# Splitting the last expert's second product into two column halves with their own sums, and swapping two PSUM banks between turns

## The chip, the core and the metric

The kernel runs on one core of a Trainium2 chip. The core has a matrix engine (TensorE; PE in the rows, PEld for its weight loads), a vector engine (VectorE; DVE), a scalar engine (ScalarE; ACT), a general engine (GpSimd; POOL) and a synchronising engine that issues most transfers (SyncE; SP). The metric is device time in microseconds (us) of one execution; the profile's rows are times inside one profiled execution, counted from the start of its span. Matmul results land in PSUM, which has eight banks of 2 KB in each of 128 partitions; a bank holds 512 fp32 columns.

## The reference, cut to what matters

Three stages follow one another: attention over (2, 8, 768, 64) with sink tokens and a window of 128; a dense feed-forward layer of 512 to 2048 to 512 on the 1536 tokens; and a routed layer with eight experts, of which each token goes to one. Only the last stage is touched here:

```python
logits = x @ w_gate
expert_idx = np.argmax(logits, axis=1)
...
h = np.maximum(np.einsum('ecd,edf->ecf', disp, w1), 0.0)
y = np.einsum('ecf,efd->ecd', h, w2)
out[i] = gate_w[i] * y[expert_idx[i], pos[i]]
```

An expert has `w1` of 512 x 1024 and `w2` of 1024 x 512, and takes at most 384 tokens.

## The kernel before, in words

Every fp32 product is made of fp32r products: an operand is cut into a high part (`h`, a rounded copy made by ScalarE) and a low part (`l`, the difference, made by VectorE), and the products high times high, high times low and low times high are summed in PSUM. The weights of the experts come from memory in pieces of 128 x 512 (L1274), are cut (L1291 or L1289 the high part, L1293 the low part) and wait in buffers named `cw`.

The routed tokens of each expert lie in a queue in memory, in units of 128. The experts are worked on one after another, as eight groups, in an order set by the number of tokens. For the first four groups the program holds arms for one, two or three units, chosen by a branch on the number of tokens; the execution profiled takes arms with two or three units. An arm is `group` (L1598):

- each unit's tokens are turned by TensorE (four transposes, `turn`, L1410) into a bank, and cut from there by ScalarE and VectorE (`x_parts`, L1416 and L1417) into `xt`. Unit 0 of the next group is turned early, while the group before is at work, into the tile `px`. Unit 1 is turned at the start of its group into `ph3`, and unit 2 into `px`; in the first group, whose units 0 and 1 were done ahead, only unit 2 is turned, into `ph3`;
- the first product (`up`, L1429) into the four tiles `ph0` to `ph3`, with ReLU and cutting (`h_parts`, L1438 and L1439) into `ht`;
- the second product (`down`, L1478) into the tiles `py0`, `py1` and `py2`, one for each unit;
- the multiplication by the gate (`out`, L1486) into `ys`, and an indirect DMA from GpSimd's queue (L1487) to the tokens' rows of the output.

The last four groups have few tokens. One runs as `lone` (one unit), and three as `half` (L1573), with at most 64 tokens each. In a half group the 128 stationary columns of a matmul are 64 high parts and 64 low parts, so that two products (with the weights' high and low part) do the work of three; the result's rows 0 to 63 and 64 to 127 must be added at the end. The steps of `half` for group gi are: the first product (L1531), 16 matmuls of 512 columns into `ph0` and `ph1`; a copy (L1534) to `hs`; `half_turn` (L1541), which turns `hs` and adds its two halves; ReLU and cutting (L1544, L1545); the second product `half_down` (L1552), 16 matmuls of 512 columns in one accumulation into one bank, `py0` or `py1` by the parity of gi; and `half_out`, in which ScalarE multiplies rows 64 to 127 by the gate into `hs` (L1561), VectorE multiplies rows 0 to 63 by the gate and adds (L1562), and GpSimd issues the output's indirect DMA (L1564). `half_next` turns the next half group's tokens into `px`.

The order of the work on every engine in this part is the order in which the code is written. The eight banks are `ph0` to `ph3`, `py0` to `py2` and `px`. `ph3`, `py1`, `py2` and `px` are opened after the routing's own four banks are closed; `ph3` takes the bank in which the first group's unit 1 was turned, `px` the bank of an earlier routing step.

## Time and profile before

| what | value |
|---|---|
| median of 3 runs | 599.1 us (596.08, 599.1, 600.12) |
| the profiled execution | 597.57 us |
| span of its rows | 595.8 us |
| TensorE matmul busy | 567.0 us (95%) |
| VectorE busy | 340.1 us (57%) |
| ScalarE busy | 288.2 us (48%) |
| GpSimd busy | 189.0 us (32%) |
[...]

The span is what the engines' rows cover; the execution's own time is 1.77 us longer. Each busy share is an average over all stages. In the page's strip of 40 slices (14.9 us each) TensorE stands at 8 or 9 tenths in every slice but the last, where it stands at 4.

### The profile page before, as it was taken

How to read it: one execution, taken by the hardware profiler on the slowest of the kernel's cores; microseconds unless marked ns; L12 is line 12 of the kernel's file. 1: busy time of each engine (PE TensorE's matmuls, PEld its weight loads, DVE VectorE, ACT ScalarE, POOL GpSimd, SP SyncE). 2: the span in 40 equal slices, each digit the busy share in tenths (PEclk: the TensorE clock that was granted, in tenths of full speed). 3: DMA queues.
4: the chain of work that ended last, by engine and by line, in shares of the span. 5: the costliest groups of instructions: out<-in, count | busy, mean ns of one | idle time of the engine just before them, and what ended most of it. 6: DMA issues, size and time to landing. Idle time of an engine off the chain costs nothing. (4 is left out here: it accounts for less than half of the span.)

```text
span 595.8 us, 11536 instructions
## 1 busy us (share of the span) xinstructions
PE 567.0 (95%) x3925; PEld 492.5 (83%) x3925; DVE 340.1 (57%) x814; ACT 288.2 (48%) x836; POOL 189.0 (32%) x304
## 2 busy tenths in 40 slices
PE   8879899999999999999999999999899999999994
PEld 7656677889888888898889889987698988988783
DVE  4999996554444344434444522475467666646992
ACT  4737576744345444444454423453434444424771
POOL 5328799722422242224222332141202010001110
PEclk9969899999999999999999999999989999999998
DMA  8979996834174022220240037562375765444940
GB/s 228 251 223 297 315 275 193 254 109 143 65 219 124 19 68 73 92 55 14 68 129 14 5 111 269 179 214 70 109 238 181 240 222 172 156 153 131 324 157 10
DMA packets 83562, 91.87 MB, mean 154 GB/s; under 512 B 42963, under 2 KB 51155, under 8 KB 83472
## 3 DMA queue, kind: packets, MB, share of 16 engines
q1 hardware_dynamic: 81488, 85.68, 46.9%
q0 software_dynamic: 1984, 5.13, 2.4%
q8 instruction: 39, 0.64, 0.4%
q14 instruction: 51, 0.42, 0.3%
HBM read 72.01 MB, written 20.09 MB: 155 GB/s over the span
## 5 line engine op out<-in xcount | busy, mean ns | idle before, releaser
L1010 PE MATMUL y<-wh,gp 128*128 128x512 f32 x360 | 131.2, 405 | 0.7 <-ACT gp L990 0.7
L992 POOL TENSOR_TENSOR gp<-g,gp 128x256 fp32r<-128x256 f32 x81 | 60.7, 749 | 189.2 <-ACT gp L990 180.9
L981 DVE TENSOR_TENSOR g<-hps,g 128x256 f32<-128x256 f32 x84 | 35.4, 422 | 109.8 <-ACT g L980 106.2
L964 PE MATMUL hps<-xth,wh 128*128 128x256 f32 x320 | 91.7, 287 | 0.4 <-DVE g L981 0.4
L964 PE MATMUL hps<-xtl,wh 128*128 128x256 f32 x320 | 90.1, 282 | 0.0
L964 PE MATMUL hps<-xth,wl 128*128 128x256 f32 x320 | 90.0, 281 | 0.0
L1293 DVE TENSOR_TENSOR cw<-craw,cw 128x512 fp32r<-128x512 f32 x128 | 84.0, 699 | 9.2 <-ACT cw L1291 8.0
L1010 PEld LDWEIGHTS y<-wh,gp 128*128 128x128 f32 x360 | 67.6, 188 | 15.3 <-ACT gp L990 1.1
L1291 ACT CAST cw<-craw 128x512 fp32r<-128x512 f32 x112 | 63.4, 621 | 23.7 <-PE py L1478 23.1
L980 ACT ACTIVATE g<-hps 128x256 f32<-128x256 f32 x84 | 32.2, 383 | 79.5 <-PE hps L964 78.3
L1010 PE MATMUL y<-wl,gp 128*128 128x512 f32 x180 | 70.4, 391 | 0.0
L1478 PE MATMUL py<-cw,ht 128*128 128x512 f32 x264 | 64.0, 398 | 0.3 <-DVE ht L1466 0.3
L964 PEld LDWEIGHTS hps<-xth,wh 128*128 128x128 f32 x320 | 60.3, 188 | 3.4 <-DVE g L981 0.9
L964 PEld LDWEIGHTS hps<-xtl,wh 128*128 128x128 f32 x320 | 60.3, 188 | 2.4
L964 PEld LDWEIGHTS hps<-xth,wl 128*128 128x128 f32 x320 | 60.6, 189 | 0.0
L1429 PE MATMUL ph<-xt,cw 128*128 128x256 f32 (+2 forms) x444 | 59.2, 295 | 1.1 <-DVE xt L1417 1.1
L1429 PEld LDWEIGHTS ph<-xt,cw 128*128 128x128 f32 x444 | 58.0, 194 | 1.4 <-DVE xt L1417 1.3
L1478 PEld LDWEIGHTS py<-cw,ht 128*128 128x128 f32 x264 | 49.0, 189 | 11.7 <-DVE ht L1466 0.9
L990 ACT CAST gp<-g 128x256 fp32r<-128x256 f32 x84 | 34.5, 410 | 30.9 <-DVE g L981 29.7
L1487 POOL DMA_INDIRECT out<-ys,gt x11 | 11.4, 1034 | 115.2 <-DVE ys L1486 109.7
L562 ACT ACTIVATE pm<-pm,mx 128x132 f32<-128x132 f32 (+1 forms) x80 | 31.6, 400 | 13.6 <-DVE mx L553 13.6
L1010 PEld LDWEIGHTS y<-wl,gp 128*128 128x128 f32 x180 | 34.0, 189 | 3.9
(222 smaller groups left out, 1007.2 us busy)
## 6 DMA issues: line engine op xcount, KB each, us to landing
craw<-in_moe_w SPq DMA_DIRECT2D x128, 256.0 KB
rawi<-in_moe_w_in SPq DMA_DIRECT2D x16, 512.0 KB
rawo<-in_moe_w_out SPq DMA_DIRECT2D x16, 512.0 KB
places<-zero SPq DMA_DIRECT2D x24, 257.0 KB
wh<-wscr SPq DMA_DIRECT2D x16, 256.0 KB
wl<-wscr SPq DMA_DIRECT2D x16, 256.0 KB
xg<-places SPq DMA_DIRECT2D x12, 257.0 KB
natv<-in_v SPq DMA_DIRECT2D x12, 256.0 KB
```

Source lines behind the costliest of these rows:

```text
L562: self.nc.scalar.activation(a, a, AF.Exp, bias=mx[:, pr, e:e + 1], accum_out=su[:, pr, e:e + 1])
L964: nc.tensor.matmul(ps, lhsT=w, rhs=x, start=(n == 0), stop=(n == len(mm) - 1))
L980: nc.scalar.activation(g, ps, AF.Copy, scale=0.01)
L981: nc.vector.tensor_tensor(out=g, in0=ps, in1=g, op=ALU.max)
L990: nc.scalar.copy(gp[:, 0], g)
L992: eng.tensor_tensor(out=gp[:, 1], in0=g, in1=gp[:, 0].bitcast(F32), op=ALU.subtract)
L1010: nc.tensor.matmul(y, lhsT=l, rhs=r, start=(start and n == 0), stop=(stop and n == len(mm) - 1))
L1291: nc.scalar.copy(h, t)
L1293: eng.tensor_tensor(out=l, in0=t, in1=h.bitcast(F32), op=ALU.subtract)
L1429: nc.tensor.matmul(self.ph[f][:, sl], lhsT=self.w[e, "a", h, k][w][:, f * P:(f + 1) * P], rhs=self.xt[:, a, k, sl], start=(m == 0), stop=( ...
L1478: nc.tensor.matmul(self.py[n], lhsT=x, rhs=w, start=(h == 0 and f == 0 and m == 0), stop=(h == self.NH - 1 and f == self.HF - 1 and m == 2))
L1487: nc.gpsimd.indirect_dma_start(out=self.A["out"], out_offset=bass.IndirectOffsetOnAxis(ap=gt[:, 1:2].bitcast(I32), axis=0), in_=ys[:], in_ ...
```

## The change

Two edits.

First, in the last group alone (`last`), the second product is made in two halves of 256 columns. The first half accumulates in the bank it had (`py0` or `py1` by parity; here `py1`), the second in `py2`, which the half groups do not use otherwise. `half_out` is parted into `half_sum`, which adds and scales the columns given to it, and the issue of the output DMA. For the last group the first half is summed before the last eight matmuls of the second half are issued, and the second half after them; one DMA still sends both. For the other half groups the lists have one element, and the instructions are those of before.

Second, in `group`, the turn of unit 1 goes to `px` and that of unit 2 to `ph3`, where it was the other way round; in the first group, unit 2 goes to `px`.

```diff
-    def half_down(self, gi, h, fs):
+    def half_down(self, gi, h, fs, cols=slice(None), bank=None):
         nc, c = self.nc, gi % 2 * P
+        py = self.py[gi % 2 if bank is None else bank]
         for f in fs:
             for m, w in enumerate(self.w[self.groups[gi][0], "b", h, f]):
-                nc.tensor.matmul(self.py[gi % 2], lhsT=self.ht[:, 0, h * self.HF + f, c:c + P], rhs=w,
+                nc.tensor.matmul(py[:, cols], lhsT=self.ht[:, 0, h * self.HF + f, c:c + P], rhs=w[:, cols],
...
-    def half_out(self, gi):
+    def half_sum(self, gi, cols=slice(None), bank=None):
         nc, Q = self.nc, P // 2
-        gt, ys, py = self.gt[gi % 4][0], self.ys[self.nout % 2], self.py[gi % 2]
-        self.nout += 1
-        t = self.hs[1]
+        gt = self.gt[gi % 4][0]
+        ys, py, t = (x[:, cols] for x in (self.ys[self.nout % 2], self.py[gi % 2 if bank is None else bank], self.hs[1]))
         nc.scalar.activation(t[0:Q], py[Q:], AF.Copy, scale=gt[Q:, 0:1])
         nc.vector.scalar_tensor_tensor(out=ys[0:Q], in0=py[0:Q], scalar=gt[0:Q, 0:1], in1=t[0:Q], op0=ALU.mult,
                                        op1=ALU.add)
...
-        self.half_down(gi, 0, range(1))
+        c = self.DM // 2
+        last = gi + 1 == len(self.groups) and len(self.py) > 2
+        banks = [(slice(0, c), gi % 2), (slice(c, 2 * c), 2)] if last else [(slice(None), gi % 2)]
+        for b in banks:
+            self.half_down(gi, 0, range(1), *b)
         self.half_turn(gi, 1)
-        self.half_down(gi, 0, range(1, HF))
+        for b in banks:
+            self.half_down(gi, 0, range(1, HF), *b)
         self.release("b", gi, 0)
         self.refill(next(go))
-        self.half_down(gi, 1, range(HF))
+        for b in banks[:-1]:
+            self.half_down(gi, 1, range(HF), *b)
+            self.half_sum(gi, *b)
+        self.half_down(gi, 1, range(HF), *banks[-1])
         self.release("b", gi, 1)
         self.refill(next(go))
+        self.half_sum(gi, *banks[-1])
         self.half_out(gi)
...
-            px = self.px if (u - u0) % 2 == 0 else self.ph[3].rearrange("p (k c) -> p k c", k=self.K)
+            px = self.px if (u - u0) % 2 else self.ph[3].rearrange("p (k c) -> p k c", k=self.K)
```

What moves on TensorE in the last half group: `py_5854` is `py1`, `py_5855` is `py2`, `ph_5853` is `ph3` and `twice` the operand of `half_turn`. The column after the arrow is the pair of operands, then the shape and the count.

```order
-L1552 MATMUL py_5854<-cw,ht 128x512 [waits DVE_49]
-L1552 MATMUL py_5854<-cw,ht 128x512
+L1553 MATMUL py_5854<-cw,ht 128x256 [waits DVE_49]
+L1553 MATMUL py_5854<-cw,ht 128x256
+L1553 MATMUL py_5855<-cw,ht 128x256 x2
 L1541 MATMUL ph_5853<-twice,hs_5556 128x64 [waits Activation_49]
 L1541 MATMUL ph_5853<-twice,hs_5556 128x64 x3
```

```order
-L1552 MATMUL py_5854<-cw,ht 128x512 x6
-L1552 MATMUL py_5854<-cw,ht 128x512 [waits DVE_49]
-L1552 MATMUL py_5854<-cw,ht 128x512 x7
...
+L1553 MATMUL py_5854<-cw,ht 128x256 x6
+L1553 MATMUL py_5855<-cw,ht 128x256 x6
+L1553 MATMUL py_5854<-cw,ht 128x256 [waits DVE_49]
+L1553 MATMUL py_5854<-cw,ht 128x256 x7
+L1553 MATMUL py_5855<-cw,ht 128x256 x8
```

Before the turn, two matmuls of 512 columns become four of 256; behind it, fourteen become twenty-eight, and the last eight of these write the second bank alone.

What moves on VectorE at the end of the same group (ScalarE's L1561 moves in the same way):

```order
 L1293 TENSOR_TENSOR cw<-craw,cw 128x512 [waits DMAHW5_49,Activation_49]
 L1545 SCALAR_TENSOR_TENSOR ht<-ph_5853,ht 128x4x64 [waits Activation_49]
-L1562 SCALAR_TENSOR_TENSOR ys_5558<-py_5854,gt_0_4871,hs_5556 64x512 [waits DMASW1_49,Activation_49]
+L1562 SCALAR_TENSOR_TENSOR ys_5558<-py_5854,gt_0_4871,hs_5556 64x256 [waits DMASW1_49,Activation_49]
+L1562 SCALAR_TENSOR_TENSOR ys_5558<-py_5855,gt_0_4871,hs_5556 64x256 [waits Activation_49]
```

One sum of 512 columns becomes two of 256, the first from `py1`, the second from `py2`.

What moves on TensorE at the start of the first group's arm, behind the branch on the number of tokens (`xg_2` are the tokens of unit 2):

```order
 L1478 MATMUL py_5554<-cw,ht 128x512 x3
 L1322 TENSOR_LOAD counts [waits DVE_49]
-L1672 COMPARE_AND_BRANCH
-L1410 MATMUL ph_5853<-ident,xg_2_4858 128x128 [waits DVE_49,DMAHW6_49,PE_49,Activation_49]
-L1410 MATMUL ph_5853<-ident,xg_2_4858 128x128 x3
+L1686 COMPARE_AND_BRANCH
+L1410 MATMUL px<-ident,xg_2_4858 128x128 [waits DVE_49,DMAHW6_49,PE_49,Activation_49]
+L1410 MATMUL px<-ident,xg_2_4858 128x128 x3
 L1429 MATMUL ph_5514<-xt,cw 128x128 x12
 L1429 MATMUL ph_5514<-xt,cw 128x128 [waits Activation_49]
```

The turn's tile changes; its place and the semaphores that it waits for are those of before, and the twelve products behind it have no wait of their own in either program.

## Rows read from the trace of the kernel before

**Rows 1.** The page, engines' busy time over the span:

```profile
span 595.8 us, 11536 instructions
PE 567.0 (95%) x3925; PEld 492.5 (83%) x3925; DVE 340.1 (57%) x814; ACT 288.2 (48%) x836; POOL 189.0 (32%) x304
```

**Rows 2.** Chain of waits in order of time, from 580: start, us, what:

```profile
579.36 2.51 DMA out<-ys,gt
...
581.91 7.11 issue
```

**Rows 3.** Timeline from 580 us: start, us, engine, line, operation, count, [idle before]:

```profile
582.15 0.59 ACT L1534 COPY hs<-ph 128x512 f32<-128x512 f32 x1
583.08 1.00 PE L1541 MATMUL ph<-twice,hs 128*128 128x64 f32 x8
583.89 3.51 PE L1552 MATMUL py<-cw,ht 128*128 128x512 f32 x14
584.53 0.42 DVE L1545 SCALAR_TENSOR_TENSOR ht<-ph,ht 128x256 fp32r<-128x256 f32 x1 [0.55 <-ACT ht L1544]
587.52 0.68 ACT L1561 ACTIVATE hs<-py,gt 64x512 f32<-64x512 f32 x1 [3.02 <-PE py L1552]
588.24 0.74 DVE L1562 SCALAR_TENSOR_TENSOR ys<-py,gt,hs 64x512 f32<-64x512 f32 x1 [3.28 <-ACT hs L1561]
589.26 0.91 POOL L1564 DMA_INDIRECT out<-ys,gt  x1 [8.98 <-DVE ys L1562]
```

**Rows 4.** Lines, shapes apart, 557 to 596 us: count, busy us, mean ns:

```profile
L1552 PE MATMUL py<-cw,ht 128*128 128x512 f32 x48 | 12.7, 406 | 0.7 <-DVE ht L1545 0.7
L1552 PEld LDWEIGHTS py<-cw,ht 128*128 128x128 f32 x48 | 8.5, 188 | 3.3 <-DVE ht L1545 1.8
L1534 ACT COPY hs<-ph 128x512 f32<-128x512 f32 x6 | 3.5, 588 | 3.2 <-PE ph L1531 2.9
L1562 DVE SCALAR_TENSOR_TENSOR ys<-py,gt,hs 64x512 f32<-64x512 f32 x3 | 2.2, 742 | 3.4 <-ACT hs L1561 3.3
L1561 ACT ACTIVATE hs<-py,gt 64x512 f32<-64x512 f32 x3 | 2.1, 686 | 4.4 <-PE py L1552 4.4
L1523 DVE TENSOR_TENSOR xt<-px,xt 128x256 fp32r<-128x256 f32 x2 | 0.8, 424 | 0.9 <-ACT xt L1522 0.9
L1522 ACT CAST xt<-px 128x256 fp32r<-128x256 f32 x2 | 0.8, 377 | 0.0
```

**Rows 5.** TensorE's timeline, first layer: products of 256 columns, single:

```profile
249.82 0.28 PE L964 MATMUL hps<-xtl,wh 128*128 128x256 f32 x1
...
250.65 0.28 PE L964 MATMUL hps<-xth,wl 128*128 128x256 f32 x1
```

**Rows 6.** Timeline, start of the first group's arm (TensorE, VectorE):

```profile
428.26 0.69 DVE L1417 TENSOR_TENSOR xt<-px,xt 128x512 fp32r<-128x512 f32 x1 [5.22 <-ACT xt L1416]
429.20 0.63 PE L1410 MATMUL ph<-ident,xg 128*128 128x128 f32 x4 [0.91 <-DVE xt L1417]
430.58 1.90 DVE L1293 TENSOR_TENSOR cw<-craw,cw 128x512 fp32r<-128x512 f32 x3
432.39 0.68 DVE L1417 TENSOR_TENSOR xt<-ph,xt 128x512 fp32r<-128x512 f32 x1
433.13 12.18 PE L1429 MATMUL ph<-xt,cw 128*128 128x128 f32 x88 [1.12 <-DVE xt L1417]
```

**Rows 7.** Timeline, third group's start, and the arm of three units:

```profile
470.27 11.41 PE L1478 MATMUL py<-cw,ht 128*128 128x512 f32 x48
477.48 1.39 DVE L1293 TENSOR_TENSOR cw<-craw,cw 128x512 fp32r<-128x512 f32 x2 [0.54 <-ACT cw L1291]
483.08 0.63 PE L1410 MATMUL ph<-ident,xg 128*128 128x128 f32 x4 [1.40 <-DVE ys L1486]
509.89 17.31 PE L1429 MATMUL ph<-xt,cw 128*128 128x128 f32 x108
510.79 0.69 DVE L1417 TENSOR_TENSOR xt<-px,xt 128x512 fp32r<-128x512 f32 x1 [1.02 <-ACT xt L1416]
```

## The prediction

> **What bounds the kernel now.** I read the page first. TensorE is busy for 567.0 of 595.8 us [rows 1]: as far as a sum over all stages can tell, what shortens TensorE's work or the few stretches in which it stands still shortens the kernel. The change touches two places of the last stage, so I then went to those.

> The first is the end. The chain of waits [rows 2] is misleading there: it goes from the last output DMA back to the one before it (579.36, 2.51 us), across 7.11 us put down to nothing. The timeline [rows 3] shows what came last. TensorE ends its fourteen matmuls at 583.89 + 3.51 = 587.40; ScalarE starts the sum 0.12 later, at 587.52; VectorE runs from 588.24 to 588.98; GpSimd starts the DMA 0.28 later, at 589.26. The DMA before it had landed at 579.36 + 2.51 = 581.87, far earlier, so the path is TensorE, ScalarE, VectorE, GpSimd, and every microsecond taken out of it comes off the end. From 589.26 to 595.8 nothing depends on the change except by its start. ScalarE stands idle for 3.02 us before its sum, VectorE for 3.28: room for work brought forward.

> The second place is the turns at the start of each group's arm [rows 6, 7].

> **The sum over the column halves.** Behind TensorE's end two instructions of 512 columns, 0.686 and 0.742 us [rows 4], become two of 256. No row has L1561 or L1562 at 256 columns, so I bound them. Each can cost as little as half (0.343 and 0.371; 0.71 us saved together) or as much as before (nothing saved). Between them I take the step that other instructions show from 512 to 256 columns, reading PSUM on the same engine. ScalarE: a copy of 512 takes 588 ns, one of 256 377 [rows 4], 0.21 less. VectorE: L1417 with 512 takes 0.69 [rows 6], L1523 with 256 424 ns [rows 4], 0.27 less. That makes 0.48 and 0.47 us, and saves 0.21 + 0.27 = **0.48 us**. The waits between them stay: 0.12, 0.04 and 0.28.

> This holds if the first half's sum is out of the way. The last eight matmuls, all of the second half, run behind it for 8 x 0.12 = 0.95 us. Counted from the end of the first half's matmuls, the first ScalarE part ends at 0.12 + 0.48 = 0.60, the first VectorE part at 0.60 + 0.04 + 0.47 = 1.11. The second ScalarE part may start at 0.95 + 0.12 = 1.07 and VectorE's second at 1.59: neither waits. The slack is 0.47 and 0.48 us; a first pair later than that would take the gain back by as much as it is later. VectorE's last work before it ends at 584.53 + 0.42 = 584.95, so nothing else is in the way.

> [...]

> **The second product in halves.** Sixteen matmuls of 512 columns become thirty-two of 256, each with its own weight load. In the larger part, fourteen of them, 13 steps and one duration (0.41 [rows 4]) fill 3.51 us [rows 3]: a step is 0.24. The first layer has products of 256 columns, also one weight load each, at the same operand types: eight of them from 249.82 to 250.65, seven steps of 0.83 / 7 = 0.119 us, 0.28 us for one [rows 5]. Twenty-eight take 27 x 0.119 + 0.28 = 3.49 us instead of 3.51. The first four take as long until the next may start as the first two did (4 x 0.119 = 0.48), and the turn that follows at 583.08 waits for `hs`, ready at 582.74, and for them. **Nothing**, then: the columns streamed are the same. The second half needs the same `ht`, ready at 584.95, before TensorE comes to it, and a bank whose last reader was done long before. The bound on the bad side is a weight load that isn't hidden: a step of 0.188 [rows 4] instead of 0.119 makes 31 x 0.069 = 2.1 us more. I take the other end, since rows 5 are the same shape in the same alternation.

> **The swapped banks.** In the first group TensorE idles 0.91 us before the turn of unit 2 [rows 6]: VectorE's L1417 ends at 428.95 reading unit 1's turn, in the bank that `ph3` takes. Now the turn goes to `px`, in another bank. But the twelve products behind the turn need the low part that the same L1417 makes, and have no wait of their own, so the turn's wait must cover it: it asks for the same count of VectorE's instructions in both programs. Even if it came 0.9 us sooner, the low part of unit 2 comes at 432.39 behind VectorE's row of cuts (1.90 us from 430.58), and TensorE would wait for it at 433.13 all the longer. So nothing. In the later groups unit 1 now turns into `px`, which is read later than `ph3` was. Since a group's arms meet in one count, the wait asks for more than that reader: in the arm taken, for the first weight cut behind the first unit's output, which runs at 477.48 (the first of two in 1.39 us), while TensorE is in the second product until 470.27 + 11.41 = 481.68 [rows 7]. That covers it by 3.5 us; without it, the turn would come when the cut ends. The 1.40 us of idle time before 483.08 stand against a VectorE instruction that ends after both counts, so I take them for something else, and leave them. In the arm of three units unit 2 turns into `ph3`; it is read by 511.48, and the fourth group of products, which writes `ph3`, starts 36 or more products after 509.89, at over 0.119 each: after 514. Nothing.

> **Sum.** -0.48 + 0 + 0 = -0.5 us: the span goes from 595.8 to 595.3, the profiled execution from 597.57 to 597.1. That execution lies 1.5 us below the median of the three runs; put on the median, 599.1 - 0.5 = **598.6 us**.

> **The rivals.**

> *Weight loads show (slower).* In the last group every halved matmul waits for its weights. It decides from a step of 0.137 us on: there 27 steps have grown by the 0.48 saved. At 0.188 the end moves by 2.1 - 0.5 = +1.6 us: 600.7. For it: TensorE loads the same weights twice as often. Against it: rows 5, and the 512-column matmuls, whose steps of 0.24 hold a load of 0.188 beside the streaming. [...] Chance 0.06.

> *No gain at the end.* The halved sums cost nearly what the whole ones do, or the first pair is late: 599.1. For it: L1561 and L1562 take a per-row scale and 64 rows, and are dearer than the copies used. Chance 0.14.

> *The swap works.* Unit 2's turn comes up to 0.9 us sooner and VectorE's low part with it: 597.7. Against it: VectorE goes from its row of cuts (430.58 + 1.90 = 432.48) straight into that low part. Chance 0.06.

> *The code's place moves.* The idle time before 483.08 has no data behind it; a stall of this sort could come or go, 1.4 us either way: 597.2 or 600.0. The code ahead of the last group has the same instructions as before. Chance 0.06.

> The forecast keeps 0.68.

> **Range and chances.** The runs shown lie between 3.0 below and 1.0 above their median, far more than any term here. The bottom of the range is the lowest of them with the forecast's gain, 596.08 - 0.48 = 595.6, which holds the two gaining rivals too; its top is the slow rival's end and half a microsecond of spread, 601.2: **595.6 to 601.2**. About 1%, 6 us, is what a measurement can tell from no change; no case reaches it: within 1% 0.94, faster 0.03, slower 0.03, the rest for what isn't priced, such as a fall of the granted clock.

> **What would show it.** In the profile after: L1561 and L1562 twice each with 64x256 at about 0.48 us, the first pair before TensorE's last matmul ends; 128x256 matmuls at 0.119 us; from TensorE's end to the DMA's start 1.4 us instead of 1.86; the same gaps at the turns. Matmul steps over 0.137, a first pair that delays the second, or a turn at 428.4 would make it wrong.

## The result, and the profile after

The changed kernel takes 606.26 us (median of 4 runs, 605.8 to 607.83); the kernel before, run beside it, 597.97 (4 runs, 596.08 to 600.12). The ratio is 1.0131, 95% interval 1.0089 to 1.0173: slower by 1.3%, about 8 us, where 0.5 us of gain was forecast. The profiled execution after took 606.06 us. Ratios here and below are over fast runs alone, while the medians of the kernel before hold all its runs (of those beside the first four experiments 3 of 25 count as slow, beside the last three 4 of 19), so a ratio need not be the quotient of the medians beside it.

The page of the changed kernel: the span, and each engine's busy time (share of the span), instructions.

```profile
span 604.3 us, 11567 instructions
PE 571.1 (95%) x3941; PEld 498.3 (82%) x3941; DVE 339.8 (56%) x815; ACT 288.2 (48%) x837; POOL 188.5 (31%) x304
```

The span is 8.5 us longer and TensorE busy 4.1 us more, though the work is the same: part is waiting, part slower work (mean granted TensorE clock 0.970, before 0.982). TensorE's rows at the turns show where (start, us, engine, line, operation, [idle before <- what ended it]); [rows 6, 7] are those of before.

```profile
428.37 1.09 PE L1410 MATMUL px<-ident,xg 128*128 128x128 f32 x4 [0.90 <-DVE xt L1417]
429.11 17.15 PE L1429 MATMUL ph<-xt,cw 128*128 128x128 f32 x108
446.10 0.60 PE L1410 MATMUL px<-ident,xg 128*128 128x128 f32 x4
...
471.54 11.41 PE L1478 MATMUL py<-cw,ht 128*128 128x512 f32 x48
487.45 1.12 PE L1410 MATMUL px<-ident,xg 128*128 128x128 f32 x4 [4.50 <-DMA craw<-in_moe_w]
488.22 16.67 PE L1429 MATMUL ph<-xt,cw 128*128 128x128 f32 x108
```

At the third group's start the idle time before the turn is 4.50 us instead of 1.40, and the 108 products behind it take 16.67 us; the same count took 12.89 in the second group of this trace. The windows give the granted clock there (start:end, length, busy time and count of each engine, then clock, DMA share, GB/s):

```profile
483.00:487.00 4.00, 0.00 (x0) 0.00 (x0) 0.75 (x1) 0.00 (x0) 1.28 (x3) 0.88 0.59 203
487.00:497.00 10.00, 9.55 (x47) 9.55 (x48) 3.82 (x7) 3.43 (x7) 0.00 (x0) 0.53 0.40 133
497.00:507.00 10.00, 10.00 (x79) 9.67 (x78) 6.43 (x14) 5.39 (x13) 0.00 (x0) 1.00 0.32 109
```

TensorE stands still for 4.50 us, then works for some nine at a granted clock of 0.50 (the mean from 487 to 496 us; 0.53 to 497), then at 1.00 again. The traces give this clock as a share of full speed and nothing in GHz: the 1.2 GHz of the expectations below is this 0.50.

Measured from the start of one row to the start of the next, the 8.5 us divide so. The first group's turn begins 0.83 us earlier (428.37 against 429.20). From it to the early turn for the second group (446.10 against 445.15) it takes 1.78 longer, in part at the low clock (mean 0.74 from 425 to 445 us against 0.91 before). From there to the second group's second product it takes 0.32 longer. From that product's start to the third group's turn it is 15.91 us against 12.81: 3.10. From there to TensorE's end it is 4.29 more, 4.17 of them within the third group's turn and first 108 products. From TensorE's end to the span's it is 0.16 less. -0.83 + 1.78 + 0.32 + 3.10 + 4.29 - 0.16 = 8.50.

What ended the idle time isn't a weight's DMA, although the chain of waits says so:

```profile
482.49 4.17 DMA craw<-in_moe_w
486.66 0.79 issue
487.45 1.12 PE px L1410 x4
```

The turn doesn't wait for that DMA: it waits for its tokens and for a count of VectorE, whose last instruction before the turn ended at 483.05 + 0.75 = 483.80:

```profile
483.05 0.75 DVE L1486 TENSOR_SCALAR ys<-py,gt 128x512 f32<-128x512 f32 x1 [1.24 <-issue]
```

The branch ahead of the turn has rows of its own, by its line, on TensorE's queue of instructions (PEldq; minimum/median/maximum ns, first and last start in us). Before:

```profile
L1672 PEldq COMPARE_BRANCH  x3: 78/298/5072, 477.3 to 482.8; - x3
```

After:

```profile
L1686 PEldq COMPARE_BRANCH  x3: 70/293/3597, 478.6 to 482.6; - x3
```

The three are, in order, the jump from the second group's arm to the place where the arms join, the compare that leads past the third group's arm of three units, and the compare that enters its arm of two. The second is the long one: 5.07 us before, 3.60 after. After the change the last of the three has begun at 482.6, when TensorE's queued products still run (to 471.54 + 11.41 = 482.95): all of the 4.50 us come behind the jump.

While such a jump lasts, the DMA queue q8 moves code ("instruction": packets, MB, share of 16 engines). Before, in the 1.5 us from 477.5:

```profile
q8 instruction: 2, 0.03, 16.1%
```

After, first from 478.9 to 482.6 us, then from 482.6 to 486.1:

```profile
q8 instruction: 1, 0.02, 2.6%
...
q8 instruction: 1, 0.02, 3.2%
```

The code did move, although the same work stands in it. In the kernel before, the first product behind the turn waits for two engines, and the second wait is an instruction of its own (in the third group's arm it runs at 483.1 us for 51 ns; after, L1429 has none from 482 to 489). The views show the first of the turn's four transposes and the first product, with their waits, in the second group's arm of two:

```
 L1410 MATMUL ph_5853<-ident,xg_1_4860 128x128 [waits DMAHW7_49,DVE_49]
...
 L1429 MATMUL ph_5514<-xt,cw 128x128 [waits DVE_49,Activation_49]
```

With the swapped banks the turn's own wait covers VectorE's part, and the product waits for ScalarE alone:

```
 L1410 MATMUL px<-ident,xg_1_4860 128x128 [waits DMAHW7_49,DVE_49]
...
 L1429 MATMUL ph_5514<-xt,cw 128x128 [waits Activation_49]
```

That takes one instruction out of each of three arms ahead of the third group's arm of two, which begins at TensorE's instruction 7936 instead of 7939.

### The profile page after: what moved, and what is told of

Same layout as the page of the kernel before. It is cut to its first block, busy times and chain, and to the rows that moved or that the text cites. A ratio compares the mean times of both kernels' runs of the same rounds, so it can differ in the third digit from the quotient of the medians.

```text
span 604.3 us, 11567 instructions
## 1 busy us (share of the span) xinstructions
PE 571.1 (95%) x3941; PEld 498.3 (82%) x3941; DVE 339.8 (56%) x815; ACT 288.2 (48%) x837; POOL 188.5 (31%) x304
## 4 chain that ended last, share of the span: by engine, by line
PE 73%; DVE 9%; issue 5%; DMA 5%; ACT 4%; POOL 2%; SPq 0%; another core or an unknown queue 0%; POOLq 0%; DVEq 0%; ACTq 0%
PE y L1010 19%; PE hps L964 18%; PE ph L1429 11%; PE py L1478 8%; PE ops L625 4%; PE sps L540 3%; PE lps L1095 2%; DMA craw<-in_moe_w 2%; PE qps L512 1%; PE py L1553 1%; PE pps L589 1%; DVE cw L1293 1%; DVE cvt L897 1%; DMA out<-ys,gt 1%; PE px L1410 1%
## 5 line engine op out<-in xcount | busy, mean ns | idle before, releaser
L1429 PE MATMUL ph<-xt,cw 128*128 128x256 f32 (+2 forms) x444 | 65.5, 315 | 0.0
L1429 PEld LDWEIGHTS ph<-xt,cw 128*128 128x128 f32 x444 | 64.5, 215 | 0.1
```

The source lines that it names most:

```text
L1429: nc.tensor.matmul(self.ph[f][:, sl], lhsT=self.w[e, "a", h, k][w][:, f * P:(f + 1) * P], rhs=self.xt[:, a, k, sl], start=(m == 0), stop=( ...
```

## The experiments

Three theories: CODE, as above; BANK, the turn into `px` waits for a later reader; HALVES, the halved product and sum cost the time. Code is moved by transposes written into an arm that these data don't take: nothing that runs is changed.

**The swap alone.** The kernel before with

```diff
-            px = self.px if (u - u0) % 2 == 0 else self.ph[3].rearrange("p (k c) -> p k c", k=self.K)
+            px = self.px if (u - u0) % 2 else self.ph[3].rearrange("p (k c) -> p k c", k=self.K)
```

> The kernel before with the swapped banks alone; the last expert's second product and its sum stay whole. Three theories. CODE: the turn at the third group's start comes late because the place in TensorE's code to which its branch leads lies, in the changed kernel, at the very end of one block of code, so that the next block is loaded only behind the branch, and TensorE's standing still then brings the low clock. The swap alone moves the code by the same three instructions, so this run should look like the changed kernel: 4.5 us of idle time before that turn, the clock at 1.2 GHz behind it, 606 us. BANK: the turn into px waits for a later reader than the turn into ph3 did: also 606. HALVES: the halved columns and their extra code make the loss: this run is at the time before, 598.

605.12 us against 599.0; ratio 1.0101 (1.0065 to 1.0138). The row of the turn and the products in its trace:

```profile
487.31 1.11 PE L1410 MATMUL px<-ident,xg 128*128 128x128 f32 x4 [3.38 <-issue]
488.08 17.27 PE L1429 MATMUL ph<-xt,cw 128*128 128x128 f32 x108
```

The swap alone brings the loss, without any halves: 6.1 us between the medians against 8.3 for the whole change. HALVES falls. The idle time is 3.38 us rather than 4.5, and no DMA is named.

**The changed kernel, code moved by 16 instructions.**

```diff
                 self.turn(gi, u, px)
+                if gi == 2 and n == 3 and u == 1:
+                    for _ in range(8):
+                        self.nc.tensor.transpose(px[:, 0, :], self.xg[gi % 2][u][:, 0:P], self.ident)
                 self.x_parts(gi, u, px)
```

> The changed kernel with 8 more transposes in the third group's arm of three units, which does not run on these data: nothing that runs is changed, but all code behind that arm lies 16 instructions of TensorE further on. CODE: the idle time before the third group's turn (4.50 us) goes to 0.3 or less and the stretch at 1.2 GHz behind it, which took 4.2 us, goes with it: 606.3 - 4.5 - 4.2 = 597.6. BANK: the waits are the same, so 606.3. HALVES: 606.3.

600.36 us against 599.0; ratio 1.0028 (0.9988 to 1.0068).

```profile
483.28 0.63 PE L1410 MATMUL px<-ident,xg 128*128 128x128 f32 x4 [1.34 <-DVE ys L1486]
483.67 12.90 PE L1429 MATMUL ph<-xt,cw 128*128 128x128 f32 x108
```

Eight transposes that never run give most of the loss back, and what is left isn't clear of noise. The banks are still swapped, the waits are the same, and BANK falls. But 1.34 us of idle time stay where 0.3 or less was expected, and the time is 2.8 us over the expected one.

**The kernel before, code moved by 16 and by 252.** The same edit in the kernel before, with `range(8)` and with `range(126)`.

> The kernel before with the same 8 transposes in the arm that does not run. CODE: the branch of 5.07 us becomes one of some 3.6, as at the second group, and the 1.40 us of idle time before the third group's turn goes: 598.0 - 1.4 = 596.6. BANK and HALVES: no change, 598.0.

> The kernel before with 126 transposes in the arm that does not run: the code behind it lies 252 instructions further on, which against blocks of 256 is 4 back, about where the change put it (3 back). CODE: as in the changed kernel, 4.5 us of idle time before the third group's turn and a stretch at 1.2 GHz behind it: 598.0 + 3.1 + 4.2 = 605.3. BANK and HALVES: 598.0, since neither is in this kernel.

With 16: 599.45 against 599.0, ratio 1.0008 (0.9971 to 1.0044), idle time 1.08 us: the expected gain did not come. With 252: 606.83 us, ratio 1.0136 (1.0066 to 1.0206), without anything of the change in it:

```profile
484.98 1.01 PE L1410 MATMUL ph<-ident,xg 128*128 128x128 f32 x4 [4.54 <-DMA craw<-in_moe_w]
485.64 16.38 PE L1429 MATMUL ph<-xt,cw 128*128 128x128 f32 x108
```

So the place of the code makes the loss. The miss with 16 mends the theory. In that trace, and in the one with the changed kernel moved by 16, two packets come at the jump (it takes 4.75 and 4.99 us). The author's reading, which no row shows as such: when the jump to the join enters a block, the next block begins to load; where the compare then leads into the block behind that one, both have to come. What follows for this kernel, and what the later runs try: the target should lie in the very next block, and far from its end.

**Halves alone.** The changed kernel with the swap undone (the first diff, backwards).

> The changed kernel with the swapped banks undone: the last expert's second product and its sum stay in halves. CODE: the code ahead of the third group stands as before, so its turn idles for 1.1 to 1.4 us and the clock stays up there: the loss of 7 to 8 us is gone. What is left is the end: VectorE's last sum ends 1.0 us behind TensorE's last matmul instead of 1.58, but GpSimd starts the output's DMA 0.77 us behind it instead of 0.28: a gain of 0.1 us in all, 597.9 against 598.0. HALVES (that the halved columns cost the time): 606.

599.95 us against 599.35; ratio 0.9991 (0.9952 to 1.0031): neither gain nor loss to be seen, as CODE has it. In its trace the clock fell behind 1.64 us of idle time: 0.50 from 487 to 493 us, 16.03 us for the 108 products.

**Moved by 174.** The kernel before, `if gi == 1 and n == 3 and u == 1` and `range(87)` in the same place: the third group's compare stands near the start of a block, and leads into the next one, 82 instructions ahead of its end.

> The kernel before with 87 transposes in the second group's arm of three units, which does not run: the code behind lies 174 instructions further on, so that the third group's branch leads into the block that is loaded anyway because it comes next, and 80 instructions ahead of that block's end. CODE: one block less to wait for, the branch takes 3.6 us instead of 5.07, the 1.40 us of idle time before the turn go, and the block behind it comes just in time: 596.6 against 598.0. If the idle time has another cause than the loads (a wait for VectorE's sum, as the profile names it): 598.0.

597.56 us against 599.35; ratio 0.9956 (0.9923 to 0.9988), faster than the kernel before: 1.8 us between the medians, 1.4 expected. The turn has no idle time, and the longest jump ahead of it is 3.06 us:

```profile
483.51 0.60 PE L1410 MATMUL ph<-ident,xg 128*128 128x128 f32 x4
483.86 12.90 PE L1429 MATMUL ph<-xt,cw 128*128 128x128 f32 x108
...
L1675 PEldq COMPARE_BRANCH  x3: 70/297/3057, 479.3 to 482.8; - x3
```

**A copy on GpSimd.** The halves without the swap, and in `half_x`

```diff
         nc.gpsimd.tensor_copy(self.gt[gi % 4][0].bitcast(I32), self.xg[gi % 2][0][:, DM:DM + 2].bitcast(I32))
+        if gi + 1 == len(self.groups):
+            nc.gpsimd.tensor_copy(self.gt[(gi + 1) % 4][0].bitcast(I32), self.gt[gi % 4][0].bitcast(I32))
```

> The halves without the swapped banks, and a copy of the last group's gates on GpSimd right behind the one that makes them, so that GpSimd has waited for its own result long before the output's DMA and that DMA waits for VectorE alone, as in the kernel before. If the 0.49 us that GpSimd lost come from the wait that stands in an instruction of its own, the DMA starts 0.28 us behind VectorE and the end is 0.57 us shorter than before: 597.4 against 598.0. If they come from elsewhere (GpSimd's own code being loaded): 0.77 us and 597.9.

599.48 us against 599.35; ratio 0.9996 (0.9955 to 1.0038), which tells nothing of half a microsecond. The trace does. The end of the changed kernel:

```profile
592.49 3.57 PE L1553 MATMUL py<-cw,ht 128*128 128x256 f32 x28
...
595.23 0.47 ACT L1561 ACTIVATE hs<-py,gt 64x256 f32<-64x256 f32 x1 [2.13 <-PE py L1553]
595.73 0.47 DVE L1562 SCALAR_TENSOR_TENSOR ys<-py,gt,hs 64x256 f32<-64x256 f32 x1 [2.17 <-ACT hs L1561]
596.10 0.47 ACT L1561 ACTIVATE hs<-py,gt 64x256 f32<-64x256 f32 x1 [0.40 <-PE py L1553]
596.60 0.47 DVE L1562 SCALAR_TENSOR_TENSOR ys<-py,gt,hs 64x256 f32<-64x256 f32 x1 [0.39 <-ACT hs L1561]
597.84 0.91 POOL L1569 DMA_INDIRECT out<-ys,gt  x1 [9.00 <-DVE ys L1562]
```

GpSimd's own wait there, by its line, and the same end with the copy:

```profile
L1569 POOLq EVENT_SEMAPHORE  x1: 6652/6652/6652, 590.5 to 590.5; - x1
```

```profile
593.94 0.47 DVE L1564 SCALAR_TENSOR_TENSOR ys<-py,gt,hs 64x256 f32<-64x256 f32 x1 [0.38 <-ACT hs L1563]
594.69 0.91 POOL L1571 DMA_INDIRECT out<-ys,gt  x1 [8.51 <-DVE ys L1564]
```

In the changed kernel the DMA starts 597.84 - 597.07 = 0.77 us behind VectorE, with the copy 0.28, as in [rows 3]. The split made the DMA wait for a third semaphore, GpSimd's own; VectorE's wait then stands in an instruction ahead of the DMA (the one of 6.65 us), and the DMA comes half a microsecond behind it.

**Halves, copy and the 174 together; the whole change with the 174; and with the copy as well.**

> The halves, the copy on GpSimd and the code moved on by 174 instructions together, without the swapped banks. CODE: no idle time before the third group's turn (1.4 us) and 0.57 us at the end: 598.0 - 1.4 - 0.57 = 596.0. If neither holds: 597.9.

> The changed kernel, swapped banks and halves as they are, with 87 transposes in the second group's arm of three units, which does not run. CODE: no idle time before the third group's turn and no fall of the clock there, GpSimd still 0.77 us behind VectorE at the end: as the kernel before with the same shift (597.6), less 0.1: 597.5, so that the swapped banks cost nothing by themselves. BANK (the wait for the later reader of px costs time once the loads are out of the way): the turn still idles, 599 or more.

> The same with the copy of the last group's gates on GpSimd as well: the whole change with both of its side effects taken away. 597.5 - 0.49 = 597.0; like the version without the swapped banks (596.5) within what the runs can tell. BANK: 598.5 or more.

The first: 596.51 us against 599.35, ratio 0.9941 (0.9909 to 0.9972), the fastest against the kernel before that was tried. The second: 597.24 against 598.55, ratio 0.999 (0.9955 to 1.0024). The third: 596.78, ratio 0.9987 (0.9956 to 1.0018). With or without the swap the turn has no idle time and the clock stays at 1.00 behind it, so no cost of the swapped banks themselves is to be seen. That the changed kernel with both repairs beats the kernel before isn't shown: the interval holds 1.

**Near the block's end.** The kernel before, as with the 174, `range(117)`.

> The kernel before with 117 transposes in the second group's arm of three units: the third group's branch leads into the block that comes next, as with 174, but only some 20 instructions ahead of its end instead of 80. CODE: the branch takes 3.6 us and the turn comes without idle time, but after it and some five products TensorE stands still until the next block has come: loaded and usable some 4.9 us after the branch's end (482.63 to 487.45 in the changed kernel) less 2.4 us of work, so 2.4 us of idle time inside the row of 108 products, and 600 us or more, with the clock's fall behind it 604. If only the branch counts and not how much of its block is left: 597.6, as with 174.

602.9 us against 598.55; ratio 1.0106 (1.004 to 1.0172).

```profile
479.69 0.60 PE L1410 MATMUL ph<-ident,xg 128*128 128x128 f32 x4
480.04 0.75 PE L1429 MATMUL ph<-xt,cw 128*128 128x128 f32 x5
483.87 15.44 PE L1429 MATMUL ph<-xt,cw 128*128 128x128 f32 x103 [3.08 <-issue]
```

The turn comes at once, and after five products TensorE stops for 3.08 us (2.4 expected) in the middle of a row of products that wait for nothing. The changed kernel with the 174 and the copy does so too, after 37 products and for 0.39 us:

```profile
482.05 4.46 PE L1429 MATMUL ph<-xt,cw 128*128 128x128 f32 x37
486.90 8.69 PE L1429 MATMUL ph<-xt,cw 128*128 128x256 f32 x71 [0.39 <-issue]
```

Counted in the two programs, both stops are at TensorE's instruction 8195. In the changed kernel the stop before the turn is at 7939, 256 earlier: the ends of two neighbouring blocks. So in the kernel before the third group's arm begins with the first instruction of a block, two blocks on from the jump, and in the changed kernel with the last three of the block ahead of it.

## Why the prediction was wrong

**The swapped banks: the step that failed.** It was put at nothing; the swap alone, as it was built, cost 6.1 us (605.12 against 599.0). "So nothing" was right for data and banks, in every group: the first group's turn waits 0.90 us for L1417 with the swap, 0.91 without, and the third group's turn comes without idle time once the code lies well. It was wrong for the code. The step left the 1.40 us before 483.08 as "something else". 1.10 of them were the end of a jump of 5.07 us, of which TensorE's queued products covered 3.97 (from the compare's start at 477.71 to 481.68); the other 0.30 lie between the jump's end and the turn. What stood exposed there could grow: with three instructions less the jump was covered, but the block behind it came late, and the idle time was 4.50.

**The rival "The code's place moves"** named this mechanism, with a chance of 0.06 and two errors. Its price, 1.4 us either way, was the stall seen, not what a block that is asked for late can cost: 3.1 us more, and 4.2 of work at the low clock behind it. And "the code ahead of the last group has the same instructions as before" holds for the work, not for the waits that are instructions. The branch's own row, 5.07 us on TensorE, would have shown the price of a jump.

In these traces a jump during which q8 moved one packet took TensorE 3.02 us (moved by 234) to 4.00 us (the changed kernel, into the second group), and one during which it moved two 4.75 us (the kernel before moved by 16) to 5.31 us (the halves alone). Where the target lay near its block's end, the block behind it came too late: a stop of 3.08 us five products behind the turn, with one packet of q8 from 479.5 to 483.9. That a block is 256 instructions rests on the 16 KB of a packet and the 256 instructions between the two stops.

**The clock** had no term. Behind 3.1 to 4.5 us of idle time it fell in all four profiles that have it (0.53 from 487 to 497 us in the changed kernel, 0.52 there with the swap alone, 0.59 from 485 to 495 with the 252, 0.57 from 484 to 492 with the 234). Behind 1.1 to 1.6 us it fell in two of five (the halves alone, 1.64, and with the copy, 1.24: 0.66 from 485 to 495 in both) and not in three (before, 1.40; 1.34; 1.08: 1.00 over the ten microseconds behind). So the kernel before may well pay this in some of its runs, as part of its spread; this is argued, not shown: 17 of its 50 runs beside the 174 versions lie above 600 us, none of the 40 runs of the four 174 versions does (highest 599.22). What decides at equal idle time stays open. The first group's low clock, 1.78 of the 8.5 us between the two profiles, doesn't go with the change: the mean clock from 425 to 445 us was 0.74 in three profiles with the swap and 0.91 in two, and 0.66 to 1.00 without it.

**The sum over the halves** was right in mechanism: 0.47 us for each of the four parts (0.48 and 0.47 expected), the first pair out of the way. VectorE ends 1.01 us behind TensorE instead of 1.58: 0.57 gained, 0.48 forecast (the rest is ScalarE, which starts 0.04 instead of 0.12 behind TensorE). The unforeseen term is GpSimd's third wait: the 0.28 us that the prediction kept between VectorE and the DMA became 0.77, so that the DMA came 1.78 us behind TensorE instead of 1.86. With the copy on GpSimd it was 1.30.

**The second product in halves: nothing**, as said: 28 matmuls in 3.57 us instead of 14 in 3.51. A step is (3.57 - 0.29) / 27 = 0.121 us, and the rival of weight loads that show is out.

## What to carry to other kernels

Behind a branch, look at the branch's own time and at how far the target lies from the end of its block of code; a change that only drops a wait moves all code behind it. Here the branch took 5.07 us before and 3.60 after, and a target some 22 instructions ahead of its block's end brought a stop of 3.08 us, one 82 ahead none. Code that never runs is a cheap test for this: if some transposes in an arm not taken move the time, the time is not in the data. An idle time that no data explains is a term, with a price that can grow, and TensorE's clock may fall behind it (here to 0.50 behind 4.50 us, and not behind 1.08).

## What the runs showed of the hardware

Three instructions less, or 126 transposes that never run, are worth some 7 us of 600 here (6.1 and 7.8 between the medians): in the changed kernel 3.1 us more of standing still, and 4.2 for some nine microseconds of work at a granted clock of 0.50. The profile puts such idle time down to what happened to come last: VectorE's sum at 1.08 to 1.64 us, a weight's DMA at 4.50 and 4.54, "issue" at 3.38 and 3.08. And a third semaphore on a GpSimd DMA cost 0.49 us here (it started 0.77 us behind VectorE, with the copy 0.28), since VectorE's wait stood in an instruction ahead of it, of 6.65 us.
